# Where tiles lie and when loads and products are issued: five edits to a fused attention, gated attention and mixer kernel on one core

## The chip, the core and the metric

The kernel runs on one core of a Trainium2 chip. The core has a matrix engine (TensorE, PE in the rows), VectorE (DVE), ScalarE (ACT), GpSimd (POOL) and SyncE (SP), which issues the transfers. TensorE writes only to PSUM, eight banks of 2 KB in each of 128 partitions. The time is that of the device for one execution, in microseconds (us).

## The reference, cut to what matters

```
x   = local_attention(q, k, v, mem_k, mem_v)  # 4 x 768 tokens, 8 heads of 64; chunks of 32, 16 left, 8 right, 8 memory keys
logits = x @ w_gate                           # 4 experts, the best 2 of them weighted by a softmax
for e in range(4):
    q, k, v = x @ wq[e], x @ wk[e], x @ wv[e]
    a = softmax(mask_causal(q @ k.T / 8))     # 768 x 768 per batch
    out += weight[e] * (a @ v @ wo[e])
xt = out.transpose(0, 2, 1)
u  = out + (xt @ U @ V).transpose(0, 2, 1)    # U: 768 x 32, V: 32 x 768
return u + relu(u @ w_ch1) @ w_ch2            # 512 -> 2048 -> 512
```

## The kernel before

The program is one straight list of instructions. The author writes tiles and operations in Python; a scheduler decides the order on each engine, sets the semaphores, and hands out the buffers of the tile pools. Each engine then takes its own list strictly in that order, so an instruction that waits holds up all that stand behind it on its engine. `tc.issue_after(x)` keeps what is issued inside it behind `x` on the same engine. A tile with a tag shares the tag's buffers, and must wait until the last reader of the buffer's former tile is done.

Matrix products are made in three parts (high by high, high by low, low by high) to reach the accuracy, so nearly every operand is split into a high part (ScalarE casts) and a low part (VectorE subtracts). The weights `w1` and `w2` (`w_ch1`, `w_ch2`) and the matrices `mU`, `mV` come as 64-bit words: `decode` loads them (tile `raw64`, `raw` in the rows), scales one half on ScalarE (L129), and does three bit operations on VectorE (L130 to L132); `decode_split` then casts on ScalarE (L137) and subtracts on VectorE (L138).

Four stages follow each other:

1. A start (about 0 to 66 us): the first half batches of local attention. `local_load` fetches `q_t`, `k_t` and `v_t` of one unit (a batch, a pair of heads, half the sequence), `local_scores` makes scores `s` and their exponentials, `local_turn` transposes them (`tp`) and copies the result to SBUF (`at`, L470, by ScalarE for the first of a unit's two turns), `local_values` multiplies by the values. `load_mixer` decodes `mU` and `mV`.
2. Four batches of expert attention, each in 12 rounds (`ROUNDS`). A round `rnd` makes the scores `sc` of two experts and one block of 128 queries (L579 and L580, and a product L582 with a bf16 identity that adds the causal mask), takes maximum (VectorE), exponential (ScalarE) and the scaling by sum and gate (GpSimd, VectorE at the end), and in the next round transposes them (`tpc`, L633), copies them (`ath`) and multiplies by the values (`t`, L705). Local attention of the next batch and its projections (`pqk`, `pv`) are spread over the rounds as fillers. After a batch the mixer runs: `mix_turn` (`pyt`), `mix_down`, and `mix_up`, which makes `pz` and the tile `z` and stores it to `zs` in DRAM.
3. In the last batch there is no next one, and its fillers are an early part of the last multi-layer product: weights `w1` fused with `wo` (`fuse_w1`, `w1p`), the products `ph` (`gemm1`) and `po` (`gemm2`) for the first two chunks of 512 tokens and four of sixteen `w2` blocks, and factors of two pairs of blocks. `save_part` copies a finished `po` to a tile `o` and stores it to `part`. They are written in generators (`early`, `fill`) from which each round takes some steps.
4. After the attention: the same products for the other four chunks with the remaining weights decoded beside them (441 to 527 us), then a long run of products `acc` by a scheme of seven factors (527 to 815 us), then an end.

PSUM holds, in the attention, two banks of tag `lt` (pool `pt2`, which lasts the whole kernel), one each of `ts` and `q`, and two double banks of tag `c`, which scores and transposes of the expert attention share. In stage 4 the same space holds `po0` to `po3` and two banks `fu`.

The lines that set when the first weights are fetched are in the loop over batches, in the last batch:

```
if r == 0:
    close_local()
    with tc.issue_after(hold['q', PRO + 1]):
        load_wt()
    fuse = fuse_w1(ps, 0, TL)
if r < 6:
    with tc.issue_after(hold['q', PRO + 1]) if r < 2 else ExitStack():
        take(fuse, 2)
```

`hold['q', n]` is the load of the n-th unit's `q_t`; PRO is 6. They are written in the last batch, but nothing else keeps them back, so the scheduler issues their first transfers on SP right behind load 7 at the start of the kernel: two of `woT` and six of `w1`, as many as the buffers take.

## Time and profile before

| | |
|---|---|
| median of 3 runs | 838.53 us (836.74 to 841.04) |
| the profiled execution, its own time | 840.29 us |
| its span | 838.5 us |
| TensorE matmul busy | 803.5 us (96%) |
| TensorE weight loads busy | 720.8 us (86%), beside the matmuls |
| VectorE busy | 631.1 us (75%) |
| ScalarE busy | 497.5 us (59%) |
| GpSimd busy | 152.7 us (18%) |
| mean granted TensorE clock | 0.994 of full |

The busy times are shares of one span in which stages with different limits follow each other; the rows below are therefore cut by stage. Matmuls overlap, and the end of each is modelled, so a matmul's own duration is longer than its distance to the next start.

### The profile page before, as it was taken

To read this page: it belongs to the slowest core of one execution; us is meant where nothing else is said; L and a number is where in the kernel's file an instruction comes from. 1 tells how busy PE (TensorE), PEld (TensorE's weight loads), DVE (VectorE), ACT (ScalarE), POOL (GpSimd) and SP (SyncE) were. 2 spreads that over 40 slices of the span, in tenths; PEclk is the share of its full clock that TensorE was granted. 3 is DMA by queue.
4 is the path that set the end of the run, shared out by engine and by line. 5 is a ranking of instruction groups with operands and counts; after the bars stand their busy time and mean duration, and the time that the engine had idled before them with its cause. 6 is when DMAs were issued, how large, how long until landed. Compare 5 with 4: busy or idle time off the path is not lost.

```text
span 838.5 us, 17962 instructions
## 1 busy us (share of the span) xinstructions
PE 803.5 (96%) x6396; PEld 720.8 (86%) x6396; DVE 631.1 (75%) x1999; ACT 497.5 (59%) x1464; POOL 152.7 (18%) x239
## 2 busy tenths in 40 slices
PE   7889999999999998899989999999999999999997
PEld 5778989989989897787768888999999999999996
DVE  4597777777777767889656899989668496784956
ACT  5588766777676755656443566655555465654642
POOL 1354353435334334321100000000000000000000
PEclk9999999999999999999999999999999999999999
DMA  9844422433323101343206743300203012030211
GB/s 291 246 123 139 140 81 73 138 109 114 95 72 122 51 2 57 101 140 132 76 20 220 230 160 138 102 26 31 96 2 126 1 52 76 1 127 1 76 51 51
DMA packets 38377, 81.54 MB, mean 97 GB/s; under 512 B 4368, under 2 KB 7952, under 8 KB 37520
## 3 DMA queue, kind: packets, MB, share of 16 engines
q1 hardware_dynamic: 38288, 80.39, 30.0%
q8 instruction: 51, 0.84, 0.4%
q14 instruction: 38, 0.31, 0.1%
HBM read 64.64 MB, written 15.73 MB: 96 GB/s over the span
## 4 chain that ended last, share of the span: by engine, by line
PE 70%; DVE 12%; DMA 11%; ACT 4%; issue 3%; SPq 1%; POOL 0%; DVEq 0%; ACTq 0%; POOLq 0%
PE acc L1001 22%; PE ph L294 13%; PE t L705 7%; PE pqk L499 7%; DMA raw<-in_w 4%; PE s L440 3%; PE pv L539 3%; PE tpc L633 3%; PE sc L579 3%; PE po L310 2%; PE sc L580 2%; PE tp L468 2%; DMA part<-o 1%; DMA zf<-zs 1%; DMA raw<-in_wqk 1%
## 5 line engine op out<-in xcount | busy, mean ns | idle before, releaser
L1001 PE MATMUL acc<-xhi,sw 128*128 128x256 f32 x1008 | 189.1, 282 | 0.2
L1001 PEld LDWEIGHTS acc<-xhi,sw 128*128 128x128 f32 x1008 | 159.6, 189 | 5.3 <-ACT xhi L919 0.6
L1001 PE MATMUL acc<-xlo,sw 128*128 128x256 f32 x504 | 139.3, 282 | 0.2 <-DVE xlo L920 0.2
L916 DVE TENSOR_TENSOR sx<-t 128x256 f32<-128x256 f32 x180 | 67.8, 419 | 67.0 <-ACT t L909 67.0
L909 ACT ACTIVATE t<-ph 128x512 f32<-128x512 f32 x72 | 43.0, 597 | 100.0 <-PE ph L294 100.0
L1001 PEld LDWEIGHTS acc<-xlo,sw 128*128 128x128 f32 x504 | 95.5, 190 | 2.4 <-DVE xlo L920 0.4
L613 POOL TENSOR_SCALAR ac<-ac,su,g 128x128 f32<-128x128 f32 (+5 forms) x92 | 67.6, 743 | 155.5 <-DVE su L611 57.9
L919 ACT CAST xhi<-sx 128x256 fp32r<-128x256 f32 x205 | 74.5, 406 | 21.1 <-DVE sx L916 18.9
L591 ACT ACTIVATE ac<-sc,nmc 128x128 f32<-128x128 f32 (+5 forms) x96 | 60.4, 633 | 41.2 <-DVE nmc L606 29.7
L447 ACT ACTIVATE a<-a,nm 128x96 f32<-128x96 f32 x192 | 69.9, 367 | 18.1 <-DVE nm L444 17.5
L920 DVE TENSOR_TENSOR xlo<-sx,xhi 128x256 fp32r<-128x256 f32 x205 | 77.1, 418 | 2.8 <-ACT xhi L919 2.0
L294 PE MATMUL ph<-zh,wp_l 128*128 128x512 f32 x192 | 61.0, 398 | 0.9 <-ACT zh L282 0.9
L294 PE MATMUL ph<-zh,wp_h 128*128 128x512 f32 x192 | 60.8, 394 | 0.0
L440 PE MATMUL s<-k_t,q_t 128*128 128x96 f32 x384 | 54.0, 276 | 4.9 <-DVE nm L444 3.4
L452 POOL TENSOR_TENSOR a<-a,rs 128x288 f32<-128x288 f32 x64 | 42.6, 667 | 81.9 <-DVE rs L451 38.6
L440 PEld LDWEIGHTS s<-k_t,q_t 128*128 128x128 f32 x384 | 49.5, 195 | 8.1 <-DVE nm L444 5.4
L294 PE MATMUL ph<-zl,wp_h 128*128 128x512 f32 x176 | 56.1, 394 | 0.0
L633 PE MATMUL tpc<-ident_s,ac 128*128 128x128 f32 x336 | 52.4, 277 | 3.8 <-ACT ac L591 1.3
L579 PE MATMUL sc<-kl,qs 128*128 128x384 f32 (+2 forms) x144 | 51.0, 354 | 3.3 <-ACT ath L636 0.9
L444 DVE CUSTOM_DVE_ANT_0 a<-s,band_s 128x96 f32<-128x96 f32 x192 | 39.7, 251 | 15.1 <-PE s L440 14.3
L606 DVE TENSOR_REDUCE nmc<-sc 128x1 f32<-128x512 f32 (+2 forms) x48 | 39.0, 818 | 12.9 <-PE sc L582 12.4
L705 PE MATMUL t<-ath,vt 128*64 128x128 f32 x672 | 46.1, 276 | 2.1 <-DVE ath L636 1.4
(187 smaller groups left out, 1979.7 us busy)
## 6 DMA issues: line engine op xcount, KB each, us to landing
raw<-in_w SPq DMA_DIRECT2D x64, 256.0 KB, 3.3
q_t<-in_qT SPq DMA_DIRECT2D x32, 384.0 KB, 3.3
k_t<-in_kw SPq DMA_DIRECT2D x32, 288.0 KB, 3.8
v_t<-in_vw SPq DMA_DIRECT2D x32, 288.0 KB, 3.1
part<-o SPq DMA_DIRECT2D x24, 256.0 KB, 2.5
pt<-part SPq DMA_DIRECT2D x6, 1024.0 KB, 4.8
out<-pt SPq DMA_DIRECT2D x24, 256.0 KB, 2.3
zf<-zs SPq DMA_DIRECT2D x8, 512.0 KB, 4.6
```

The costliest lines, as they stand in the source:

```text
L294: nc.tensor.matmul(p, w[f // 4][:, pr, fs], z[:, pr], start=(n == 0), stop=(n == 5))
L440: last = nc.tensor.matmul(s[:, j, :], w["q"][:, qd * 3 + j], w["k"][:, qd * 3 + j], start=True, stop=True).ins
L447: nc.scalar.activation(a[:, j, :], a[:, j, :], AF.Exp, bias=nm[:, j:j + 1], scale=-1.0, accum_out=ss[:, j:j + 1])
L579: nc.tensor.matmul(s[:, o:o + w], q, kl[b, e, hf][:, :w], start=True, stop=False)
L591: nc.scalar.activation(aa[h][:, :n], src, AF.Exp, bias=nm[:, h:h + 1], scale=1.0, accum_out=su[:, h:h + 1])
L613: (nc.vector if ending[0] else nc.gpsimd).tensor_scalar(aa[h][:, :n], aa[h][:, :n], su[:, h:h + 1], gates[b, i // 3][:, i % 3, 2 * pr + h: ...
L633: nc.tensor.transpose(tp[h][:, j * 128:(j + 1) * 128], aa[h][:, j * 128:(j + 1) * 128], ident_s)
L705: session.append(nc.tensor.matmul(*a, **kw).ins)
L916: nc.vector.tensor_tensor(x, t[:, p[0], p[1]], t[:, q[0], q[1]], op=op)
L919: nc.scalar.copy(hi, x)
L920: nc.vector.tensor_sub(lo, x, f32(hi))
L1001: ended[0] = nc.tensor.matmul(acc[n][:, m], w[:, ms], x, start=(f == FA and u == 0 and m == 0), stop=(f == NF - 2 and u == 2 and m == 1)).ins
```

## The change

Five edits, and a sixth small one that comes with them:

- **PSUM in two areas.** `Banks` holds two pools instead of one. Tags `c`, `fu`, `po2` and `po3` go to the second, all others but `lt` to the first. So in stage 4 `po0` and `po1` follow `q` and `ts`, and `fu`, `po2`, `po3` follow `c`.
- **Late raw words in the early part's place.** In stage 4 the tiles `raw64` have a pool of their own, which is opened first after the early part's pool is closed, so it lies where that pool lay; it no longer shares a pool with the other decode tiles.
- **The last z outside the score buffers.** For the last batch `mix_up` stores `z` in halves of 384 columns in the buffers of `raw64` of pool `dp0`, with two transfers for each pair of experts, where before one tile of 768 columns in the score buffers (`ac`) was stored by one transfer. The second `mix_up` of the batch before takes its PSUM from tag `q` instead of `c`, in two products, and stands in round 4 instead of 5.
- **Partial outputs by ScalarE.** In stage 4 `save_part` always copies on ScalarE; before, VectorE copied every other one.
- **Early products held back.** Of the second early chunk, the last four groups of six `po` products each (the third and fourth output block) wait behind marked transposes (`'t'`) or mask products (`'s'`) of the last batch: see `GATES`. And the first fetches of `woT` and `w1` are kept behind load 14 instead of load 7.
- In the first three blocks of queries of each half batch, the mask products of both heads stand together behind the scores of both.

```
+WIDE = ('c', 'fu', 'po2', 'po3')
+GATES = {4: ('s', 10), 5: ('t', 9), 6: ('s', 11), 7: ('t', 11)}
...
+    rawp = [None]
+
     def decode(pool, src, n, t=None, p=128, **kw):
-        raw = pool.tile([p, n, 2], U32, name="raw64", **kw)
+        raw = (rawp[0] if rawp and pool is not dp0 and rawp[0] else pool).tile([p, n, 2], U32, name="raw64", **kw)
...
     class Banks:
-        def __init__(self, pool):
-            self.pool = pool
+        def __init__(self, stack, *names):
+            self.pools = [stack.enter_context(tc.tile_pool(name=n, bufs=1, space=PSUM)) for n in names]
         def tile(self, *a, **kw):
-            return (pt2 if kw.get('tag') == 'lt' else self.pool).tile(*a, **kw)
+            tag = kw['tag']
+            return (pt2 if tag == 'lt' else self.pools[tag in WIDE]).tile(*a, **kw)
...
     def save_part(po, c, m):
         o = ea.tile([128, CT], F32, name="o", tag="o", bufs=2)
-        if m % 2:
+        if m % 2 or wp2 is not None:
             nc.scalar.copy(o, po)
...
                 for f in range(FA):
-                    gemm2(po, c, f, m, f == FA - 1, f == 0)
+                    gate = GATES.get(2 * m + f // 2) if c == NEC - 1 else None
+                    with tc.issue_after(hold[gate]) if gate else ExitStack():
+                        gemm2(po, c, f, m, f == FA - 1, f == 0)
...
-        ps = Banks(p1.enter_context(tc.tile_pool(name="ps", bufs=1, space=PSUM)))
+        ps = Banks(p1, "psq", "psc")
...
                 if last:
-                    nc.tensor.matmul(s[:, o + w - 128:o + w], identb_s, tri_s, start=False, stop=True)
+                    def mask(o=o + w - 128):
+                        hold['s', 6 * (i // 3) + 3 * (e // 2) + i % 3] = nc.tensor.matmul(s[:, o:o + 128], identb_s, tri_s, start=False, stop=True).ins
+                    if masks is None:
+                        mask()
+                    else:
+                        masks.append(mask)
...
+                masks = []
                 for h in range(2):
-                    score_mm(s[:, h], 0, b, 2 * pr + h, i, 0)
+                    score_mm(s[:, h], 0, b, 2 * pr + h, i, 0, masks)
+                for mask in masks:
+                    mask()
...
-                    nc.tensor.transpose(tp[h][:, j * 128:(j + 1) * 128], aa[h][:, j * 128:(j + 1) * 128], ident_s)
+                    hold['t', 6 * (i // 3) + 3 * pr + i % 3] = nc.tensor.transpose(tp[h][:, j * 128:(j + 1) * 128], aa[h][:, j * 128:(j + 1) * 128], ident_s).ins
...
         def mix_up(b, pr):
             qm = qms.pop((b, pr))
-            z = cw.tile([128, S], F32, name="z", tag="ac", bufs=NAC)
-            if b < B - 2 or (b, pr) == (B - 2, 0):
+            if b < B - 1:
+                z = cw.tile([128, S], F32, name="z", tag="ac", bufs=NAC)
...
-                nc.vector.tensor_add(z, p[:, 128:128 + S], yT[b, pr])
+                for hf in range(2):
+                    cs = slice(hf * HALF, (hf + 1) * HALF)
+                    z = dp0.tile([128, HALF], F32, name="z1", tag="raw64", bufs=ND0)
+                    nc.vector.tensor_add(z, p[:, 128 + hf * HALF:128 + (hf + 1) * HALF], yT[b, pr][:, cs])
+                    nc.sync.dma_start(zs[b][:, pr, cs], z)
+                return
             nc.sync.dma_start(zs[b][:, pr, :], z)
...
-                if b and r == 5:
+                if b and r == (4 if last else 5):
                     f1 = [lambda: mix_up(b - 1, 1)] + f1
...
-                        with tc.issue_after(hold['q', PRO + 1]):
+                        with tc.issue_after(hold['q', 14]):
                             load_wt()
                         fuse = fuse_w1(ps, 0, TL)
                     if r < 6:
-                        with tc.issue_after(hold['q', PRO + 1]) if r < 2 else ExitStack():
+                        with tc.issue_after(hold['q', 14]) if r < 2 else ExitStack():
                             take(fuse, 2)
...
     dpe.close()
+    rawp[0] = pass_a.enter_context(tc.tile_pool(name="dpr", bufs=1, side="right"))
     dp = pass_a.enter_context(tc.tile_pool(name="dp1", bufs=1, side="right"))
...
-        ps = Banks(p2.enter_context(tc.tile_pool(name="ps2", bufs=1, space=PSUM)))
+        ps = Banks(p2, "psp", "psf")
```

How the change moves instructions, at three places. First SP's list at the start, from the load of `q_t` number 7; before:

```order
L422 DMA q_t<-in_qT 128x768
L424 DMA k_t<-in_kw 128x576
L230 DMA d_r<-in_woT 128x256 x2
L125 DMA raw_723<-in_mU 128x384
L125 DMA raw_5232<-in_w 128x512
L125 DMA raw_5249<-in_w 128x512
L125 DMA raw_729<-in_mV 128x384
L429 DMA v_t<-in_vw 96x768 x2
L125 DMA raw_5331<-in_w 128x512
L125 DMA raw_5348<-in_w 128x512
L422 DMA q_t<-in_qT 128x768
L424 DMA k_t<-in_kw 128x576
```

And the same place in the changed kernel, whose line numbers are a few higher (L129 is the load in `decode`, L429 and L431 those of `q_t` and `k_t`):

```order
L429 DMA q_t<-in_qT 128x768
L431 DMA k_t<-in_kw 128x576
L129 DMA raw_726<-in_mU 128x384
L129 DMA raw_732<-in_mV 128x384
L436 DMA v_t<-in_vw 96x768 x2
L429 DMA q_t<-in_qT 128x768
L431 DMA k_t<-in_kw 128x576
```

The two transfers of `woT` and six of `w1` have left; they stand behind the load of unit 14, in pairs, between the loads of units 14 to 16. Second, ScalarE's list at the same time, before, from the last exponentials ahead of the decoding:

```order
L447 ACTIVATE a,ss<-a,nm 128x96 x6
L129 ACTIVATE u_s<-raw_723 128x192
L129 ACTIVATE d_t<-raw_5232 128x256
L129 ACTIVATE d_t<-raw_5249 128x256
L486 CAST xh<-t 128x384
L470 COPY at<-tp 96x384
L129 ACTIVATE d_t<-raw_729 128x192
L137 CAST w_h<-d_t 128x256
L518 ACTIVATE qs<-pqk_139 64x384
```

And in the changed kernel:

```order
L454 ACTIVATE a,ss<-a,nm 128x96 x6
L133 ACTIVATE u_s<-raw_726 128x192
L133 ACTIVATE d_t<-raw_732 128x192
L493 CAST xh<-t 128x384
L398 CAST vs<-d_t 128x192
L477 COPY at<-tp 96x384
L408 CAST v_st<-vs 32x192 x3
```

Ahead of the copy `at` there now stand the words of `mU` and `mV` and the cast `vs` of the decoded `mV`; the two pieces of `w1` are gone. Third, TensorE's list in the last two rounds of the last batch; before, from the transposes of round 10:

```order
L633 MATMUL tpc<-ident_s,ac 128x128 x8
L661 MATMUL pyt<-ident_s,yT 128x128 x6
L705 MATMUL t<-ath,vt 64x128 x8
L579 MATMUL sc<-kl,qs 128x384
...
L582 MATMUL sc<-tri_s,identb_s 128x128
L633 MATMUL tpc<-ident_s,ac 128x128 x16
```

And in the changed kernel, where L315 is `gemm2` and L299 `gemm1`:

```order
L648 MATMUL tpc<-ident_s,ac 128x128 x4
L315 MATMUL po<-hh,w2l_5606 128x512
...
L315 MATMUL po<-hh,w2h_5722 128x512
L676 MATMUL pyt<-ident_s,yT 128x128 x6
L725 MATMUL t<-ath,vt 64x128 x8
...
L590 MATMUL sc<-tri_s,identb_s 128x128
L315 MATMUL po<-hh,w2l_5606 128x512
L315 MATMUL po<-hl,w2h_5605 128x512
...
L299 MATMUL ph<-zh,wp_h_5583 128x512 x2
L648 MATMUL tpc<-ident_s,ac 128x128 x16
```

Between the two halves of the eight transposes stand six `po`, behind the second half six more, behind the last mask product six `po` and six `ph`, and six `po` two steps later, ahead of the last value products: 24 `po` and 6 `ph`, which before stood further ahead, between 363 and 414 us.

## Rows read from the trace of the kernel before

**Rows 1.** Busy time by stage: us, each engine's (instructions), clock, DMA share.

```profile
38.00:66.00 28.00, 21.39 (x175) 18.31 (x175) 25.81 (x123) 22.94 (x89) 14.38 (x28) 0.94 0.39 118
80.00:310.00 230.00, 225.88 (x2332) 208.76 (x2331) 167.38 (x671) 157.87 (x551) 92.55 (x145) 1.00 0.30 91
...
363.00:412.00 49.00, 48.62 (x285) 39.78 (x285) 42.00 (x99) 27.93 (x67) 9.12 (x12) 1.00 0.37 119
412.00:441.00 29.00, 24.21 (x202) 18.50 (x201) 15.85 (x30) 12.29 (x27) 0.00 (x0) 1.00 0.09 32
441.00:527.00 86.00, 84.53 (x439) 71.50 (x438) 73.52 (x203) 48.95 (x118) 0.00 (x0) 1.00 0.58 189
527.00:815.00 288.00, 287.95 (x2032) 269.75 (x2031) 218.31 (x572) 157.68 (x383) 0.00 (x0) 1.00 0.15 54
```

**Rows 2.** TensorE's longest wait from 0 to 80 us: total, times, longest.

```profile
PE tp L468 <- ACT at L470: 3.7, 2, 2.9
```

**Rows 3.** Timeline of ScalarE at that wait: start, duration, instruction, idle before.

```profile
37.50 0.37 ACT L129 ACTIVATE u_s<-raw 128x192 f32<-128x192 f32 x1 [2.72 <-DMA raw<-in_mU]
...
39.78 0.47 ACT L470 COPY at<-tp 96x384 f32<-96x384 f32 x1
```

**Rows 4.** Timeline of SP's issues.

```profile
27.53 0.95 SPq L230 DMA_DIRECT2D d_r<-in_woT  x2
29.64 0.33 SPq L125 DMA_DIRECT2D raw<-in_mU  x1
...
33.10 0.33 SPq L125 DMA_DIRECT2D raw<-in_mV  x1
...
92.94 0.35 SPq L422 DMA_DIRECT2D q_t<-in_qT  x1
```

**Rows 5.** VectorE's decoding of `w1`, 38 to 66 us: count, busy us, mean ns.

```profile
L132 DVE SCALAR_TENSOR_TENSOR d_t<-raw,d_t 128x256 uint32<-128x256 uint32 x4 | 2.0, 497 | 0.0
...
L131 DVE SCALAR_TENSOR_TENSOR d_t<-raw,d_t 128x256 uint32<-128x256 uint32 x4 | 1.7, 414 | 0.0
...
L130 DVE TENSOR_SCALAR d_t<-d_t 128x256 uint32<-128x256 uint32 x4 | 1.2, 289 | 0.0
...
L138 DVE TENSOR_TENSOR w_l<-d_t,w_h 128x256 fp32r<-128x256 f32 x2 | 0.8, 415 | 0.0
```

**Rows 6.** ScalarE's part of it, same stretch and columns.

```profile
L129 ACT ACTIVATE d_t<-raw 128x256 f32<-128x256 f32 x4 | 1.7, 430 | 0.8 <-DMA raw<-in_w 0.8
...
L137 ACT CAST w_h<-d_t 128x256 fp32r<-128x256 f32 x2 | 0.8, 408 | 0.3 <-DVE d_t L132 0.3
```

**Rows 7.** Timeline of TensorE: both heads' first score product, second behind a mask.

```profile
345.79 0.28 PE L579 MATMUL sc<-kl,qs 128*128 128x256 f32 x1
...
346.07 0.36 PE L579 MATMUL sc<-kl,qs 128*128 128x256 f32 x1
```

**Rows 8.** Timeline of all engines in the last batch, 354 to 358 us.

```profile
355.58 0.43 ACT L129 ACTIVATE d_t<-raw 128x256 f32<-128x256 f32 x1 [1.01 <-DMA raw<-in_w]
...
356.59 0.28 DVE L636 COPY ath<-tpc 128x128 f32<-128x128 f32 x1
...
357.19 0.62 PE L696 MATMUL pz<-v_st,qm 96*128 96x384 f32 x2 [2.58 <-ACT ac L591]
```

**Rows 9.** TensorE's waits from 412 to 442 us.

```profile
PE tpc L633 <- ACT ac L591: 1.3, 1, 1.3
PE t L705 <- DVE ath L636: 1.0, 2, 0.6
PE ph L294 <- ACT zh L282: 0.9, 1, 0.9
PE tpc L633 <- ACT ath L636: 0.8, 1, 0.8
PE tpc L633 <- DVE ac L613: 0.5, 1, 0.5
```

**Rows 10.** The chain that ended last: a run of `po` products.

```profile
398.90 3.19 PE po L310 x14
```

**Rows 11.** ScalarE's wait at its copies, 442 to 530 us, and such a copy.

```profile
ACT o L315 <- DMA part<-o: 6.5, 3, 3.7
...
L315 ACT COPY o<-po x12: 567/584/589, 381.2 to 527.5; 128x512 f32<-128x512 f32 x12
```

More of the change, by code (lines that the diff above doesn't have):

```diff
@@ L570, in tile_chunk_attention__moe_attention__mixer, with score_mm @@
         yT, a_ts, ats = {}, {}, {}
-        def score_mm(s, off, b, e, i, base):
+        def score_mm(s, off, b, e, i, base, masks=None):
             q = qs[b, e, i // 3][:, i % 3 * 128:(i % 3 + 1) * 128]
```

## The prediction

> **What bounds the kernel now.** I began with the busy time by stage [rows 1]. The reader is to see that TensorE fills nearly all of the long stages (225.88 of 230 us from 80 to 310, 48.62 of 49 from 363 to 412, 84.53 of 86 from 441 to 527, 287.95 of 288 after that), while VectorE reaches 73 to 86% of them and ScalarE 57 to 69%. So there a shorter VectorE or ScalarE instruction is worth nothing in itself. TensorE has holes in three places: 6.61 us of 28 from 38 to 66, a shorter set around 355, and 4.79 of 29 from 412 to 441. Next I read TensorE's waits there, and what ran on the engine that it waited for: that is where the change can give. A gain at 38 to 66 us is kept, because the stage after it is TensorE's own. From 527 us the order of all engines is the same before and after, so I give that stage 288 us again.
>
> The profiled execution took 840.29 us with a span of 838.5, so 1.8 us lie outside it. It is 1.76 us above the median of the runs, 838.53. I work out a difference on the profiled one and take it off the median.
>
> **Held loads at the start: -4.0 us, between -6.6 and -1.5.** TensorE's longest early wait is 2.9 us for the copy `at` [rows 2]. ScalarE could not make that copy, because it stood still 2.72 us at the words of `mU`, which had not landed, until 37.50, and then had two pieces of `w1`, a cast and more ahead of `at`, which came at 39.78 [rows 3]. SP issued `woT` at 27.53, `mU` at 29.64, `mV` at 33.10 [rows 4]. With `woT` and `w1` behind load 14 (92.94), `mU` takes the first slot, 2.1 us earlier, and `mV` the second, at 29.64 at the latest, 3.4 us earlier. The words of `mU` are then there 2.1 us sooner, so most of the 2.72 us goes. Against that, `mV`'s words come ahead of `at`. A 256-column row costs 0.43 us [rows 6]; for 192 columns I estimate 192/256 of it, 0.32, and 0.31 for the cast `vs`. They replace two pieces of 0.43, and the cast can wait for VectorE's three operations on the words, 0.289 + 0.414 + 0.497 = 1.2 us for 256 columns [rows 5], so 0.9 here. Hence `at` starts about 1.5 us earlier, not 2.1. After it ScalarE is freed of the other two pieces and two casts, 0.86 + 0.8 = 1.7 us, and VectorE of 2.0 + 1.7 + 1.2 + 0.8 = 5.7 us out of 25.81 in 28 [rows 1, 5, 6]. That is 1.5 + 1.7 = 3.2 us on the chain through `at`. The granted clock is 0.94 over these 28 us; it stands at 1.00 in the long stages. If the wait of 2.9 us becomes one of about 1, the 6% of 21 us of work, 1.3 us, mostly comes back: I take 0.8. Sum 4.0. It cannot exceed the 6.6 us of holes; it is at least the 1.5 of `at`.
>
> **The same decoding in its new place: +0.5 us, between 0 and 5.7.** Nothing is saved: four words, two splits and `woT` now run from about 93 us. There TensorE is 98% busy, VectorE has 62 us free in 230, ScalarE 72 [rows 1], and that is the cover. Without it VectorE's whole 5.7 us would show. Behind each waiting L129 stand ScalarE's exponentials and copies, and TensorE waits for those; I allow 0.5.
>
> **Mask products together: -1.0 us, between -1.9 and 0.** The score product behind a mask takes 0.36 us, the same form without 0.28 [rows 7]. The mask works on another weight and another width. Together, one such seam of two falls away for each pair: 0.08 us by 24 pairs (four batches, two pairs of heads, three blocks) is 1.9. About half of them stand beside waits, so I take half. The maxima of the first head come no later than before, since one reduction takes both heads.
>
> **Mixing of the batch before, in round 4 and by tag `q`: +0.5 us, between -3.8 and +3.** At 354 us TensorE waits 2.58 us ahead of `pz` [rows 8]. The row blames the exponentials, but what came last was VectorE's copy `ath`, 356.59 to 356.87, behind ScalarE's L129, which waited 1.01 us for its words until 355.58. The edit moves `pz` away from this spot; the value products behind it still need `ath`. So I expect the stall under another name. The transposes and copies now stand ahead of the exponentials in ScalarE's list, so the score buffers free a little later: +0.5. If the stall vanished it would give 2.58 us and some 1.2 us of the lower clock behind it (0.97 from 310 to 363); if the exponentials' wait is added to it, about as much again, 3, is lost.
>
> **Held-back products: -3.5 us, between -4.8 and +3.2.** TensorE's waits from 412 to 442 are 1.3, 1.0 (0.6 and 0.4), 0.9, 0.8 and 0.5, together 4.5 [rows 9], of 4.79 without work [rows 1]. A run of 14 `po` takes 3.19 us, 0.228 each [rows 10]. 24 `po` and 6 `ph` are put in: 30 x 0.228 = 6.8 us of work that waits for nothing. Read against the order, they stand ahead of the wait for the exponentials (1.3), one copy (0.6), the `zh` (0.9) and another copy (0.8): 3.6 us. The 0.4 and 0.5 are not covered. The work itself is no more than before: what is put in here is missing from 363 to 412. That gives 3.6 only if this stretch becomes shorter by 6.8 us. TensorE has 48.62 of 49 there, and VectorE 42.00 [rows 1]: 49 - 6.8 = 42.2, so VectorE just allows it. I take 3.5. If the stretch stays as long, the end of the batch grows by 6.8 - 3.6 = 3.2 us.
>
> Here the Trainium skill, Perfetto Trace Analysis, section Identifying the Most-Contended Engine, warns that matmul busy time misjudges the headroom, and that the weight loads' share shows it better. By that, loads of 18.50 of 29 us against 39.78 of 49 (0.81) in the stretch before would leave 29 - 18.50 / 0.81 = 6.2 us of holes, and the term could be -5 instead of -3.5. The products there have other shapes, so the trace bears this out only in part.
>
> **Raw words early, partial outputs on ScalarE: -1.0 us, between -1.5 and +1.5.** Stage 441 to 527 has 1.47 us without TensorE work, and no more can be gained. ScalarE takes on eight more copies of 0.58 us, 4.7 us, in a stage where it has 37 free; VectorE, at 73.52 of 86, loses as many. But all copies now wait for the transfer of `o` two before, on the engine which already waits 6.5 us for that, 3.7 at the longest [rows 11]. Behind it stand decoding and the casts for TensorE. The early raw words work against that: six of them can land before the batch is over.
>
> **At nothing:** the PSUM areas and the halves of `z`. `po` takes over banks whose last readers are done within the first products of the stage, and runs of `po` [rows 10] cover two more transfers. Without that cover a late last `zs` would show as a wait ahead of the first `ph`; I count it in the +1.5 above.
>
> **Sum:** -4.0 + 0.5 - 1.0 + 0.5 - 3.5 - 1.0 = -8.5 us. The profile would be 831.8 us, the median 838.53 - 8.5 = 830.0.
>
> **Rivals.**
> - The stall at 354 goes as well, since `pz` no longer stands among transposes and values: -3.8 instead of +0.5, so 825.7 us. For it: the row blames `ac`, and its place changes. Against: `ath` came last.
> - The moved decoding is not hidden: +4 more, 834.0 us. For it: ScalarE's waits for raw words are seen twice, 2.72 and 1.01 us [rows 3, 8]. Against: the free time of [rows 1].
> - The last batch is bound by VectorE's chain of maxima and sums, and 363 to 412 doesn't shrink: +3.2 instead of -3.5, so 836.7 us, no change that can be told. For it: VectorE's 42.00 of 49, with dependences.
> - It becomes slower: each of six `w1` loads, now among expert attention at full load, stops ScalarE for as long as `mU` did, 2.72 us [rows 3], and TensorE feels each: 16.3 us more, so 846 us. It decides (over 842.7) from (842.7 - 830.0) / 6 = 2.1 us per load. For it: ScalarE's list is strict. Against: the DMA share there is 0.30, below the 0.39 at the start [rows 1], and the loads are issued far ahead of their first use.
>
> **How the numbers follow.** About 0.5%, 4.2 us, is what a measurement of this kernel can tell from no change: faster is below 834.3, slower above 842.7. Chances: the forecast 0.53 (827 to 834), the stall that goes 0.13, decoding not hidden 0.16, the last batch VectorE's 0.11, slower 0.07. Faster: 0.52 of the forecast, 0.13, and half of the third case, since 834.0 is at the bound, 0.08, together 0.73. Same: the other half, 0.11 and the rest, 0.20. Slower 0.07. The range reaches from the gain of the first rival with 2.7 us of its own spread, 823.0, to the VectorE case with 1.8 more, 838.5. That leaves out the slower case and about one in ten at the edges.
>
> **What would show it right or wrong.** Right: the 2.9 us wait for `at` falls to about 1, and VectorE and ScalarE have no 256-column words from 38 to 66; these come at 93 to 125 us and TensorE's waits from 80 to 310 grow by less than 1 us; a stall of over 2 us stands ahead of the value products near 350; from the last round's transposes to the end of the batch TensorE's idle time falls from 4.8 to about 1.2 us, and the stretch before is 6 to 7 us shorter; 527 to 815 stays at 288. Wrong: ScalarE waits of over 2 us for the words of `w1` near 100 with TensorE waiting behind them; a wait of VectorE's `nm` or `nmc` ahead of scores in the last batch where products were taken out; ScalarE's waits for `part` well above 6.5 us with TensorE waiting for `hh` or a decoded weight; a long first `ph` wait for the last `z`.

## The result, and the profile after

The changed kernel takes 832.54 us (median of 5 runs, 828.88 to 834.68) against 841.04 for the kernel before in the same session: a ratio of 0.9909, interval 0.9885 to 0.9933, or 5.6 to 9.7 us less (the two medians alone give 0.9899). Forecast were 8.5 less, a ratio of 0.990. One profiled execution further below, that of e10, was a slow one (granted clock 0.984, 9.1 us over the median of its others) and is left out of all means.

The profiled executions lie further apart, 840.29 and 828.88 us. To see where, I matched each TensorE instruction of one trace with the same one of the other and compared the distances between them (start times from TensorE's timeline, worked out, not rows of a view):

| stretch, from and to | before, us | after, us | change | forecast |
|---|---|---|---|---|
| start to the first expert value product `t` | 66.79 | 61.24 | -5.6 | -4.0 |
| next 28 `t`, then 56 more (90 to 127 us) | 23.73 + 36.73 | 23.67 + 38.07 | +1.3 | +0.5 |
| up to the last batch (three quarters of the `t`) | 203.78 | 203.59 | -0.2 | -1.0 |
| last batch, to the last `t` | 101.33 | 98.59 | -2.7 | +0.5 - 3.5 |
| to the first `acc`, same work | 92.20 | 88.03 | -4.2 | -1.0 |
| the `acc` run | 303.28 | 303.10 | -0.2 | 0 |

The first row holds some luck: of the 5.6 us, 3.4 lie between the first and the hundred-and-first score product `s` (51.89 and 48.52 us). Nine other profiles below, whose program is the same there (but for one pair of masks in e3), took 49.7 to 53.0 for it. With their mean (50.8, the changed kernel's own included) instead of 48.5 the table sums to 9.3 us, and with 38.6 in place of 38.07 (the mean of the eight with the same loads) to 8.8, which is inside the measured interval.

The stages of the changed kernel by engine, with the columns of [rows 1], cut at its own times. The first line is cut at the same times as before, and holds 260 TensorE instructions instead of 175, since the changed kernel is further on there:

```profile
38.00:66.00 28.00, 25.59 (x260) 22.64 (x260) 22.38 (x119) 24.04 (x100) 16.10 (x32) 0.94 0.32 103
80.00:310.00 230.00, 224.91 (x2331) 208.40 (x2330) 170.18 (x680) 156.48 (x544) 91.51 (x141) 1.00 0.31 97
363.00:404.00 41.00, 40.95 (x244) 33.94 (x243) 36.14 (x85) 24.65 (x57) 10.05 (x12) 1.00 0.32 103
404.00:436.00 32.00, 31.48 (x240) 25.43 (x238) 18.25 (x36) 13.50 (x29) 0.00 (x0) 1.00 0.34 114
436.00:513.00 77.00, 77.00 (x407) 66.08 (x406) 67.90 (x190) 49.06 (x118) 0.00 (x0) 1.00 0.57 190
```

TensorE's idle time fell from 6.61 to 2.41 us in the first line, from 4.79 to 0.52 at the end of the batch, and from 1.47 to nothing in the last. The start, in ScalarE's timeline (compare [rows 3]) and SP's issues (compare [rows 4]):

```profile
34.10 0.38 ACT L133 ACTIVATE u_s<-raw 128x192 f32<-128x192 f32 x1 [1.14 <-DMA raw<-in_mU]
35.09 0.38 ACT L133 ACTIVATE d_t<-raw 128x192 f32<-128x192 f32 x1 [0.61 <-DMA raw<-in_mV]
...
36.92 0.35 ACT L398 CAST vs<-d_t 128x192 fp32r<-128x192 f32 x1 [1.09 <-DVE d_t L136]
37.18 0.47 ACT L477 COPY at<-tp 96x384 f32<-96x384 f32 x1
```

```profile
26.39 0.33 SPq L129 DMA_DIRECT2D raw<-in_mU  x1
26.92 0.33 SPq L129 DMA_DIRECT2D raw<-in_mV  x1
```

ScalarE's 2.72 us for `mU` became 1.14, but 0.61 for `mV` and 1.09 for the cast `vs` were added ahead of `at`; the prediction had counted the second alone. Of the 3.4 us by which `u_s` starts earlier, 1.3 stand already at the load of `q_t` number 7 (25.48 and 24.19 us), before the two lists part. TensorE's wait for `at` fell from 2.9 only to 2.1, not to 1:

```profile
PE tp L475 <- ACT at L477: 2.9, 2, 2.1
```

The profiles of the experiments show that this fall is not the edit's. The longest wait for `at` is 1.7 us in e1 and 2.1 in e9, whose loads are early, and 0.8 to 3.1 us in the nine others with held loads. First e1, then e2 (total, times, longest):

```profile
PE tp L475 <- ACT at L477: 2.5, 2, 1.7
```

```profile
PE tp L475 <- ACT at L477: 3.9, 2, 3.1
```

In the last batch the stall stands under another name, as forecast. VectorE's and TensorE's timelines at 350 us:

```profile
351.55 0.29 DVE L134 TENSOR_SCALAR d_t<-d_t 128x256 uint32<-128x256 uint32 x1 [0.60 <-ACT d_t L133]
351.76 0.42 DVE L135 SCALAR_TENSOR_TENSOR d_t<-raw,d_t 128x256 uint32<-128x256 uint32 x1
352.09 0.28 DVE L651 COPY ath<-tpc 128x128 f32<-128x128 f32 x1
```

```profile
352.43 0.44 PE L725 MATMUL t<-ath,vt 128*64 128x128 f32 x4 [2.24 <-DVE ath L651]
```

And the waits of TensorE from 404 to 436 us, which in [rows 9] were five of 0.5 to 1.3:

```profile
PE tpc L648 <- ACT ath L651: 0.3, 1, 0.3
PE t L725 <- DVE ath L651: 0.2, 1, 0.2
```

From 436 us to the first `acc` TensorE has no wait left. The kernel before had these there, besides the one for `zh` in [rows 9]:

```profile
PE po L310 <- ACT o L315: 0.7, 2, 0.4
PE po L310 <- DVE o L317: 0.4, 1, 0.4
PE w1p L252 <- DVE w_l L138: 0.3, 1, 0.3
```

### The profile page after: what moved, and what is told of

Same layout as the page of the kernel before. It is cut to its first block, busy times and chain, and to the rows that moved or that the text cites. A ratio compares the mean times of both kernels' runs of the same rounds, so it can differ in the third digit from the quotient of the medians.

```text
span 827.1 us, 17950 instructions
## 1 busy us (share of the span) xinstructions
PE 800.4 (97%) x6395; PEld 721.2 (87%) x6396; DVE 625.8 (76%) x1994; ACT 501.6 (61%) x1472; POOL 152.8 (18%) x239
## 4 chain that ended last, share of the span: by engine, by line
PE 84%; DVE 7%; DMA 4%; ACT 3%; issue 1%; POOL 0%; SPq 0%; DVEq 0%; ACTq 0%; POOLq 0%
PE acc L1022 24%; PE ph L299 16%; PE po L315 8%; PE t L725 7%; PE pqk L506 6%; PE pv L546 4%; PE tpc L648 3%; PE s L447 3%; PE sc L586 3%; PE w1p L257 2%; PE sc L587 2%; PE tp L475 2%; DMA raw<-in_mV 1%; DMA raw<-in_wqk 1%; DVE a L451 1%
## 5 line engine op out<-in xcount | busy, mean ns | idle before, releaser
L603 ACT ACTIVATE ac<-sc,nmc 128x128 f32<-128x128 f32 (+5 forms) x96 | 60.4, 633 | 38.6 <-DVE nmc L621 27.2
L299 PE MATMUL ph<-zh,wp_l 128*128 128x512 f32 x192 | 60.9, 398 | 0.0
L299 PE MATMUL ph<-zh,wp_h 128*128 128x512 f32 x192 | 60.7, 394 | 0.0
L299 PE MATMUL ph<-zl,wp_h 128*128 128x512 f32 x176 | 56.0, 394 | 0.0
L586 PE MATMUL sc<-kl,qs 128*128 128x384 f32 (+2 forms) x144 | 49.3, 347 | 2.4 <-ACT ath L651 1.5
```

Source lines behind the costliest of these rows:

```text
L299: nc.tensor.matmul(p, w[f // 4][:, pr, fs], z[:, pr], start=(n == 0), stop=(n == 5))
L586: nc.tensor.matmul(s[:, o:o + w], q, kl[b, e, hf][:, :w], start=True, stop=False)
```

## The experiments

All kernels compute the whole reference. The ratio is to the kernel before, run beside them on the same chip; e1 to e8 undo one edit of the changed kernel.

| run | ratio | interval |
|---|---|---|
| the changed kernel | 0.9909 | 0.9885 to 0.9933 |
| e1, loads behind load 7 | 0.9911 | 0.9879 to 0.9944 |
| e2, products not held | 0.9936 | 0.9910 to 0.9963 |
| e3, masks apart | 0.9926 | 0.9900 to 0.9953 |
| e4, copies shared | 0.9936 | 0.9904 to 0.9968 |
| e5, raw words in the shared pool | 0.9952 | 0.9933 to 0.9971 |
| e6, one PSUM pool | 0.9978 | 0.9958 to 0.9998 |
| e7, z in the score buffers | 0.9920 | 0.9895 to 0.9946 |
| e8, mixing in round 5 | 0.9890 | 0.9868 to 0.9913 |
| e9, before with PSUM areas alone | 1.0041 | 1.0020 to 1.0062 |
| e10, words behind the copy | 0.9872 | 0.9840 to 0.9904 |
| e11, mixing in round 5, loads behind 20 | 0.9906 | 0.9882 to 0.9931 |
| e12, e10 and e11 together | 0.9920 | 0.9892 to 0.9948 |

The interval is some 2 us to either side, so the lengths of single stretches carry most of the verdicts. Where the program is the same, no wait is near and the granted clock is the same, they repeat within 0.1 us: the first 28 `t` took 23.66 to 23.76 us in all profiles. There is one profile for each kernel.

**e1**

```
-                        with tc.issue_after(hold['q', 14]):
+                        with tc.issue_after(hold['q', PRO + 1]):
```
(and the same for `fuse`). 

> The changed kernel with one edit undone: the first fetches of woT and w1 stand behind load 7 again. My theory: the copy at waits for mU again, so the first value product of the expert attention starts 3.5 to 4 us later than in the changed kernel (61.2 there), and the stretch from 85 to 123 us gives back the 1.3 us by which it grew; the whole is 2 to 3 us longer, a ratio to before of 0.9935 to 0.995. Rival: most of the 5.4 us found before 61 us are chance of the first transfers, since 1.8 us of them already stand at 38 us, before anything differs; then the whole stays within 1 us of the changed kernel, 0.990 to 0.992. Second rival: the moved decoding costs as much as it frees; then the first stretch is 3 us longer, and 85 to 123 gives all of it back.

Measured: from the first `s` to the first `t` 61.2 us. The three profiles with early loads (before, this and e9) have a mean of 60.8 (59.7 to 61.4), the ten with held loads 58.2 (56.0 to 60.4): 2.5 us, of a stretch that scatters by as much. Cut at the start of the awaited copy `at`, it shows where these come from. From the first `s` to `at` the means are 34.5 and 34.2 us, so no earlier `at` is seen. From `at` to the first `t` they are 26.2 (25.6 to 27.0) and 24.0 (23.5 to 24.7), and here the two groups don't overlap: 2.3 us. The reason that `at` stays stands in the timelines of SP and ScalarE, as means of the same profiles. With held loads SP issues `mU` 1.25 us behind the load of `k_t` number 7 instead of 3.05, but the transfer then takes 8.3 us to land instead of 6.9, so its words come 0.4 us sooner. From `u_s` to `at` it takes 3.1 us instead of 2.6.

From 85 to 123 us it takes 36.74 us, as before, where eight profiles with the loads behind load 14 took 38.1 to 39.3, mean 38.6: 1.9 us are paid back. The spread of these eight is ScalarE's wait for the words of `w1`. In the changed kernel's profile there is none; in the other seven one of 0.28 to 1.17 us, and with it taken off each of them takes 38.10 to 38.13. The longest is that of e3, which took 39.29:

```profile
ACT d_t L133 <- DMA raw<-in_w: 1.2, 1, 1.2
```

The last batch took 100.5 us in this profile, 1.9 more than the mean under e2, at a mean granted clock of 0.949 against 0.965; that the edit does this isn't shown. The whole is that of the changed kernel: as built, this edit is worth nothing that can be measured. The second rival comes nearest, and the first has its part: of the 5.6 us in the table, 3.1 are more than these means show.

**e2**

```
-GATES = {4: ('s', 10), 5: ('t', 9), 6: ('s', 11), 7: ('t', 11)}
+GATES = {}
```


> The changed kernel without the held-back products: the po products of the second early chunk stand where they did before. My theory: the stretch from the round-6 values to the middle of the last rounds becomes 6 to 7 us longer, and the holes of the last two rounds come back, 4 to 5 us; the whole is 4 to 5 us longer, a ratio of 0.9955 to 0.997. Rival: the holes came from somewhere else in the last batch (the mixing moved to round 4), so that the products only changed places; then the whole is within 1 us of the changed kernel, 0.990 to 0.992.

TensorE's waits in the last two rounds come back with the values of [rows 9]:

```profile
PE tpc L648 <- ACT ac L603: 1.3, 1, 1.3
PE t L725 <- DVE ath L651: 1.0, 2, 0.6
PE tpc L648 <- DVE ac L628: 0.5, 1, 0.5
```

The two waits for `ath` and `zh` that are still missing beside [rows 9], 0.8 and 0.9, stay covered. The last batch to its last `t` takes 101.2 us against 98.6 in the mean of five profiles with all gates (the changed kernel and e4 to e7): the held products are worth 2.6 us of the 3.5 forecast. Neither theory's number; the mechanism is the first.

**e3**

```
-                masks = []
+                masks = None
```
(with `for mask in masks or []`). 

> The changed kernel with each mask product behind its own head's scores, as before. The prediction's term: 24 seams at half of 0.08 us come back, 1.0 us, 1.9 at most, and they must show as a shorter distance between score products in batches 0 to 2 of the changed kernel. Rival, from the trace of the changed kernel: its batches 0 to 2 are no shorter than before (the parts differ by 0.02 to 0.16 us), so the seam only moved behind the pair of masks; then the times in batches 0 to 2 agree within 0.3 us and the ratio stays at 0.9905 to 0.9915.

The seam is as priced: from the first score product of a pair to what follows the second mask, 0.755 us apart and 0.681 together for 256 columns, 0.985 and 0.913 for 384, but 0.71 both ways for 128 (medians of 6 or 7 pairs). The stages of batches 1 and 2, which hold 12 pairs, are only 0.1 us shorter than before and 0.4 than here, presumably since TensorE meets the next wait sooner, which wasn't traced. The whole kernel is 1.4 us longer, inside the interval. The rival is nearer.

**e4**

```
-        if m % 2 or wp2 is not None:
+        if m % 2:
```


> The changed kernel with the copies of finished products shared again by ScalarE and VectorE in the stage from 435 to 513 us. Of the 3.9 us that this stage lost, three waits for a copy o of 0.5 to 0.6 us stood in the kernel before. Theory A: ScalarE alone copies in time, so undoing it brings these three waits back, 1.5 to 2 us. Theory B: the raw words that land early do it, and with them there the shared copies cost nothing; then the stage stays within 0.3 us of 77.8, and the ratio within 0.001 of the changed kernel's 0.991.

The stretch from the last `pz` to the first `acc` takes 78.46 us, 0.6 more than the 77.83 of the changed kernel, and no wait for a copy comes back; the 0.6 are spread over delays of at most 0.24 us between two starts. Between the theories, nearer to B.

**e5**

```
-    rawp[0] = pass_a.enter_context(tc.tile_pool(name="dpr", bufs=1, side="right"))
```


> The changed kernel without the pool of its own for the late raw words: they share a pool with the other decode tiles again, so they wait for the last z and the end of the attention's tiles. Theory A: partial copies on ScalarE do the work, raw words are there soon enough either way; the stage from the last pz to the first acc stays within 0.5 us of 77.8. Theory B: without early words, ScalarE waits for raw words as before (14.2 us in eight waits there), copies and casts behind it are late, and the stage is 2 to 4 us longer; ratio 0.993 to 0.996.

81.71 us, 3.9 more, and 1.4 more in the `acc` run. Theory B. SP's issues of raw words in the changed kernel, six of them ahead of the last stores of `part` and `zs`, then the same list here:

```profile
405.56 0.81 SPq L129 DMA_DIRECT2D raw<-in_w  x2
...
407.37 2.63 SPq L129 DMA_DIRECT2D raw<-in_w  x4
412.41 12.42 SPq L323 DMA_DIRECT2D part<-o  x2
```

```profile
407.22 18.61 SPq L323 DMA_DIRECT2D part<-o  x4
427.62 0.80 SPq L716 DMA_DIRECT2D zs<-z  x2
435.09 0.53 SPq L280 DMA_DIRECT2D zf<-zs  x1
437.31 0.80 SPq L716 DMA_DIRECT2D zs<-z  x2
438.21 2.79 SPq L129 DMA_DIRECT2D raw<-in_w  x6
```

The same six words are issued 31 to 33 us later, behind stores that wait for the last `z`. What then waits on ScalarE (first two lines; the same two are 2.3 and 4.4 us in the changed kernel) and on TensorE from 436 to 526 us:

```profile
ACT d_t L133 <- DMA raw<-in_w: 8.2, 9, 2.4
ACT hd L133 <- DMA raw<-in_w: 6.9, 6, 2.2
```

```profile
PE w1p L257 <- DVE wp_l L268: 0.8, 1, 0.8
PE acc L1021 <- ACT xhi L939: 0.7, 1, 0.7
PE w1p L257 <- ACT w_h L141: 0.6, 1, 0.6
PE po L315 <- ACT hh L307: 0.6, 1, 0.6
```

TensorE doesn't wait for the raw words themselves, but for the casts and `hh` that stand behind them in ScalarE's list.

**e6**

```
-            return (pt2 if tag == 'lt' else self.pools[tag in WIDE]).tile(*a, **kw)
+            return (pt2 if tag == 'lt' else self.pools[0]).tile(*a, **kw)
...
-        ps = Banks(p2, "psp", "psf")
+        ps = Banks(p2, "ps2")
```
(likewise `Banks(p1, "ps")`). 

> The changed kernel with one PSUM pool instead of two areas. The prediction: nothing on the path, so within 0.5 us of the changed kernel, ratio 0.990 to 0.992. Rival: po and fu then take over banks of the score buffers whose last readers are the sums of the last z, so that the first products of the stage wait for them; TensorE waits 1 to 2 us between the last pz and the first 40 products behind it, ratio 0.992 to 0.9935.

The largest undoing, and the prediction had it at nothing. From the last `t` to the first `acc` 94.6 us against 88.0: 6.6 longer. With one pool no `po` of stage 4 runs ahead of the last `pz` (96 of them by then; 114 in the changed kernel). TensorE's wait behind the last `pz` was part of it (1.0 us for `zh`), and later it waits for a copy and for `hh`:

```profile
PE po L315 <- ACT hh L307: 1.8, 1, 1.8
PE po L315 <- ACT o L320: 0.9, 1, 0.9
```

The place of the rival's wait was right for 1 us; the rest lies far behind it. The wait for `hh` is one for a transfer: ScalarE stood 2.22 us at a copy `o` until an earlier `o` had been stored to `part`, with `hh` next in its list:

```profile
501.41 0.58 ACT L320 COPY o<-po 128x512 f32<-128x512 f32 x1 [2.22 <-DMA part<-o]
501.89 0.60 ACT L307 ACTIVATE hh<-ph 128x512 fp32r<-128x512 f32 x1
```

Behind that wait the granted clock fell: its mean is 0.83 from 500 to 510 us, where the changed kernel has 1.00 through the whole stage, and ten products `po` started 0.40 us apart in the mean instead of 0.23. That is 1.7 of the 6.6 us.

**e7**

```
-                for hf in range(2):
-                    ...
-                    nc.sync.dma_start(zs[b][:, pr, cs], z)
-                return
+                z = cw.tile([128, S], F32, name="z", tag="ac", bufs=NAC)
+                nc.vector.tensor_add(z, p[:, 128:128 + S], yT[b, pr])
```


> The changed kernel with the z of the last batch in the score buffers again, one store for each pair of experts. The prediction: nothing on the path, within 0.5 us. Rival: the tiles of the next stage lie where the score buffers lay and must wait for the stores of z, so decoding, copies or the first ph start later: the stage from the last pz to the first acc is 1 to 3 us longer than 77.8, ratio 0.992 to 0.9945.

78.72 us from the last `pz` to the first `acc`, 0.9 more, and 0.5 in the `acc` run: slightly over what the prediction allowed, below the rival. SP issues the first raw words behind the last store 14.7 us after the first store of `zs`, against 12.2 in the changed kernel.

**e8**

```
-                if b and r == (4 if last else 5):
+                if b and r == 5:
```
(with the third batch's second `pz` in a score bank and one addition, as before). 

> The changed kernel with the second mixing of the third batch in round 5 again and in a double score bank. The prediction: the edit neither removes the stall of some 2.3 us that stands in that round nor costs much, +0.5 us, so undoing it gives within 0.5 us of the changed kernel; the wait for the copy ath stays, since what holds it is ScalarE's wait for the raw words of w2. Rival: it was worth 1 us or more in the last batch by freeing the score bank earlier; then the stretch from round 3 to round 6 of the last batch is 1 to 2 us longer, ratio 0.992 to 0.9935.

The wait of 2.5 us for `ac` stands ahead of `pz` again, in place of the 2.2 for `ath`; the last batch takes 97.4 us, and 98.4 in e11, which has the same undoing, against 97.8 to 99.2 (mean 98.6) in the five profiles named under e2. So the edit costs about 0.7 (0.5 was forecast), and the rival falls. The reason forecast, score buffers that come free later, doesn't show: between 326 and 376 us the changed kernel has no wait for `ac` ahead of scores. What goes with the edit is the granted clock. Its mean over the last batch is 0.98 in the five profiles with the mixing in round 5 (before, e8, e9, e11, e12) and 0.965 in eight of the nine with it in round 4 (0.949 in e1), where TensorE stays longer at the lower of its two levels, 1.2 GHz, behind the stall near 350 us. That this is the whole 0.7 isn't shown.

**e9**, the one edit alone on the kernel before.

```
+            self.pools = [stack.enter_context(tc.tile_pool(name=n, bufs=1, space=PSUM)) for n in names]
...
+            return (pt2 if tag == 'lt' else self.pools[tag in WIDE]).tile(*a, **kw)
```


> The kernel before with one edit alone: PSUM in two areas, as in the changed kernel. Theory, from the run with one PSUM pool, whose last stage was 10.4 us longer with 4.1 us of products moved into it: the banks of po0 and po1 come free before the last z, so products run there while its load is awaited. Then this edit alone takes at least the 1.1 us wait of the first ph behind the last pz, and some 4 us of products move ahead of it; the whole is 1 to 2 us shorter than before, and the waits for copies o stay (ratio 0.9975 to 0.999). Rival: the areas only matter together with the copies by ScalarE and the early raw words, which without them come into the same banks' way; then alone they give nothing (0.999 to 1.001). Second rival: they are worth 6 us by themselves (0.992 to 0.994).

None of the three: it is slower, 1.0020 to 1.0062. From the last `t` to the first `acc` 96.6 us, 4.4 longer than before. The products did move ahead of the last `pz`, and TensorE then met this, its longest wait from 436 to 526 us:

```profile
PE ph L296 <- ACT t L911: 6.0, 1, 6.0
PE po L312 <- ACT hh L304: 0.5, 1, 0.5
```

ScalarE was late for `t` since it waited 1.40 and 3.05 us for words and copied a `po` in between:

```profile
516.44 0.72 ACT L197 CAST swrl<-hd 128x256 fp32r<-128x256 f32 x2 [1.40 <-DMA hd<-in_wo]
517.52 0.59 ACT L317 COPY o<-po 128x512 f32<-128x512 f32 x1 [0.36 <-PE po L312]
...
522.41 0.43 ACT L130 ACTIVATE hd<-raw 128x256 f32<-128x256 f32 x1 [3.05 <-DMA raw<-in_w]
523.24 0.59 ACT L317 COPY o<-po 128x512 f32<-128x512 f32 x1 [0.40 <-DVE hd L131]
523.72 1.09 ACT L911 ACTIVATE t<-ph 128x512 f32<-128x512 f32 x2
```

Behind its wait of 6.0 us TensorE was at the lower clock as well (a mean of 0.57 from 523 to 531 us), and six products up to the first `acc` started some 0.43 us apart instead of 0.23: 1.4 of the 4.4 us.

So the areas let TensorE go ahead of what feeds it. From the last `t` to the first `acc` the kernel before takes 92.2 us, the changed kernel 88.0, without the early words 91.9 (e5), without the areas 94.6 (e6): with all else in place, neither of the two gains more than 0.3 us without the other. That the early words would have prevented this very wait isn't shown; the word awaited at 522 us is not one of the six, and SP issued it at 519.96.

**e10**

```
+                if ncp[0] % 2 == 0:
+                    hold['a', 6 * (i // 3) + 3 * pr + i % 3] = turned_ins[-1]
...
-                load_w2(f)
+                with tc.issue_after(hold['a', 3]) if f == 2 else ExitStack():
+                    load_w2(f)
```


> The changed kernel, but VectorE's bit operations on the third w2 block stand behind the copy ath of round 4 in its list. My theory of the stall near 350 us: the copy waits on VectorE behind an operation that waits for ScalarE, which waits for raw words; with the copy ahead, TensorE's wait of 2.2 us before the value products falls below 0.8 us, and the last batch becomes 1.5 to 2.5 us shorter. Rival: something else comes last there (exponentials, maxima), or the block's decoding is then late for the products; then a wait of 1.5 us or more stands elsewhere between 340 and 372 us, and the length up to the last transposes stays within 0.7 us.

Of this trace only the last batch is read. The wait for `ath` fell from 2.2 to 1.0 us, not below 0.8, so what held it is shown for the larger part; but waits of 0.9 and 0.7 for other copies `ath` and of 0.6 us for `ac` follow, a later stretch is 1.0 longer, and to the last `t` the batch takes 98.8 us as with the stall. The rival, in its second half: no gain in the batch. The ratio overlaps that of the changed kernel, so it settles no gain.

**e11**

```
-                        with tc.issue_after(hold['q', 14]):
+                        with tc.issue_after(hold['q', 20]):
```
(on e8). 

> The changed kernel with the second mixing of the third batch as before (round 5, score bank), and the first loads of woT and w1 behind load 20 instead of 14. The mixing: 1.2 to 1.6 us shorter from 326 to 404 us, as in the run with this alone. The loads: from 85 to 123 us, where the changed kernel took 38.1 us and its sisters with the same order 38.4 to 38.7, it takes 36.7 as before. Theory: the decoding costs that much because ScalarE and VectorE have no room at its place, and in batch 1 it falls where local attention is lighter, so at most 0.7 us of it reappear from 123 to 300 us. Rival: it costs 1.3 to 1.9 us wherever it lands. Ratio 0.986 to 0.989 by the theory, 0.9885 to 0.991 by the rival.

From 85 to 123 us 36.74, as before; from there to 155 us nothing, and in the next stretch 60.69 against the changed kernel's 58.71. The rival: the decoding costs 2 us wherever it lands among attention. TensorE's longest waits in that stretch here, of which the changed kernel has the first alone:

```profile
PE s L447 <- DVE nm L451: 0.7, 1, 0.7
PE tp L475 <- ACT at L477: 0.7, 1, 0.7
PE tpc L648 <- ACT ath L651: 0.6, 1, 0.6
```

**e12**: e10's edit on e11. 

> The run before with the copy ahead of the words of w2 as well. If both theories hold, the parts add: 3 to 5 us shorter than the changed kernel, a ratio of 0.984 to 0.987. If the copy and the mixing are one stall (in round 5 the mixing stands at the same place), they don't add, and this is no shorter than the run without the copy, 0.987 to 0.989.

98.1 us for the last batch; the wait for `ath` is 0.7, and three more of 0.6 to 0.9 stand behind it. The parts don't add. No version is shown to beat the changed kernel: e8 and e10 lie lower, with intervals that overlap its own.

## Why the prediction was right, point by point

The time, its sign and its size held, with terms that erred to both sides: too much was expected at the start (4.0 for some 2.3) and too little for the moved decoding and for stage 4 (1.0 for 4.2). That these errors cancel to within the measured interval is luck.

- **Held loads, -4.0.** Half of its mechanism didn't occur. `at` was to start 1.5 us earlier and the wait for it to fall to about 1. With held loads the wait is 2.2 us in the mean of ten profiles, with early ones 2.3 in that of three, and no earlier `at` is seen (e1). The step that failed is that an earlier issue brings the words as much earlier: they landed 0.4 us sooner, not 2.1. That gain goes into the words of `mV` and the cast `vs`, two waits (0.61 and 1.09 us in the changed kernel) where I had counted the second alone. The other half, ScalarE and VectorE freed behind `at`, was right: 2.3 us where 1.7 stood. The 0.8 us for the lower clock didn't come in the changed kernel (0.94 in that stage). Its size was right: from `at` to the first `t` the four profiles with held loads and a clock of 1.00 from 38 to 66 us (e3, e4, e11, e12) took 23.5 to 23.6 us, the five at 0.94 took 24.0 to 24.7. But the edit doesn't decide it, since e1 has 1.00 there with early loads. Two readings were off without consequence: a 192-column row already stood at 0.37 us in [rows 3] where I took 0.32, and ScalarE's share of the last long stage is 55% (157.68 of 288), not 57.
- **The decoding moved, +0.5.** Mis-sized: +1.3, and 1.9 as the mean of eight profiles. 1.3 or 1.4 of it are there without any wait for words, put down to ScalarE's and VectorE's own time; waits of TensorE for `qs` and `ath` show 0.8 of these. The rest is the slower rival's mechanism in small: where ScalarE waits for a word of `w1`, TensorE loses just as much (0.28 to 1.17 us in seven profiles, e1), but one wait in each and not six of over 2 us. Free time of 62 and 72 us in 230 did not hide 5.7, because TensorE waits for single instructions in order, not for shares. Together with the first term the edit is near nothing, which is the result of e1.
- **Masks together, -1.0.** The seam of the wider pairs shrank as read; the batches gave back most of it, and two of them became 0.1 to 0.4 shorter where 12 seams of 0.04 had been counted as 0.5.
- **Mixing in round 4, +0.5.** Right in sign and size: the stall stayed, with the cause named, and the cost is about 0.7. The reason given for it did not show; a lower granted clock over the last batch did (e8).
- **Held-back products, -3.5.** Right in place and kind; 2.6 by e2. The stretch from 363 us shrank with VectorE at 36.14 of 41, so VectorE was not the bound.
- **Raw words and copies, -1.0, "no more can be gained" than 1.5.** This step failed: the stretch to the first `acc` lost 4.2 us (with the wait of the first `ph` behind the last `pz`). I had read 1.47 us of idle time from [rows 1]. But here a stall of TensorE cost more than the gap that is shown: the five stalls of before, that first `ph` among them, add 1.09, 0.51, 0.56, 0.63 and 0.54 us to the usual distance of two starts, where the timeline shows gaps of 0.93, 0.35, 0.40, 0.35 and 0.37; by start times the whole stretch had 4.8 us more than its products' usual distances (medians by shape), after the change 0.7. The Trainium skill, Perfetto Trace Analysis, section Identifying the Most-Contended Engine, says that matmul busy time is no good measure of the headroom and points to the share of the weight loads. This case agrees: they fill 66.08 of 77 us after (0.86) and filled 71.50 of 86 before (0.83), and at the later share 71.50 / 0.86 = 83 leaves 3 us where busy time left 1.5. I had weighed that rule one stage earlier and not here.
- **PSUM areas "at nothing".** Wrong, and it is the other half of that step: without them the changed kernel loses 6.6 us (e6), without the early words 3.9 and 1.4 (e5), without the copies 0.6 (e4), without the new place of z 0.9 (e7), and the areas alone on the kernel before cost 4.4 (e9). The sum of the undoings, over 12 us, is three times what the edits give together: they don't add, and each is only worth what the others let through. Of these figures 1.7 us in e6 and 1.4 in e9 are a lower clock behind a wait. What the areas give is products to run while `zh` is awaited (18 more `po` ahead of the last `pz`); why without them the stores of `o` come so late in SP's order that ScalarE waits for one at 500 us stays open.

## What to carry to other kernels

Take a stage's headroom from the distances between the starts of its bounding engine's instructions, not from its idle time. Price edits that feed one stage (where buffers lie, when loads leave, who copies) as one term: an edit that lets the bounding engine run ahead can cost time unless what feeds it is also moved ahead, and here the undoings, added up, came to three times the whole. Work that is moved under a busy engine is not free because the others have time left on average; in an in-order list it costs where it stands ahead of something awaited. And compare a wait in several profiles before calling its change the edit's: at the start of this kernel the chance of one profile was as large as the gain.

## What the runs showed of the hardware

Between the first and the hundred-and-first product `s`, in the first 54 us, ten profiles with the same program there took 48.5 to 53.0 us, while the 28 `t` behind the start repeated within 0.1 us. Transfers of `k_t` were waited for up to 1.7 us in eight of these and not at all in two, which took 48.5 and 51.2 us, so these waits are not the whole cause. The granted clock up to the first `t` lay between 0.92 and 1.00, and not in the same order either. A change at the start is therefore read best from a stretch that begins behind this scatter, as from `at` to the first `t` above.

Three long waits of TensorE (2.2 us near 350 us in the changed kernel, 1.8 in e6, 6.0 in e9) were followed by some microseconds at the lower of its two clock levels, so they cost more than their length: 1.7 us more in e6, 1.4 in e9. The waits of at most 0.8 us in e5's stage 4 were not (its clock stayed at 1.00), and neither was one of 1.9 us near 343 us in the changed kernel, so the length of the wait alone doesn't settle it.
